# A fused S4D convolution and feed-forward kernel: the blocks of the convolution kernel dealt anew between two stretches of the program

## The chip, the cores and the metric

One core of a Trainium2 chip runs the program alone. The figure is device time in microseconds (us) of one execution, taken as the median of the executions timed; lower is better. Inside the core five engines work side by side, each through its own list of instructions in order: TensorE (PE in the profile) multiplies matrices, VectorE (DVE) and ScalarE (ACT) work element by element, GpSimd (POOL) here mostly issues transfers, and SyncE (SP) issues transfers only.

## The reference

The reference normalises an input `x` of 2048 positions by 576 channels, convolves every channel along the positions with a kernel of its own, adds a gated result to `x`, normalises again and runs a two-layer network with ReLU, 576 to 4608 to 576, all in float32:

```python
P = jnp.exp((A * dt[:, None])[:, :, None] * pos[None, None, :])
K = 2.0 * jnp.einsum("dn,dnl->dl", C, P).real       # 576 x 2048, from 128 modes a channel
...
y = jnp.fft.irfft(Uf * Kf[None, :, :], L2)[:, :, :L]
...
x = x + ga * (y + h * D_skip)
h = layernorm(x) * (1 + cb) + sb
x = x + gb * (jnp.maximum(h @ w1, 0) @ w2)
```

The six modulation vectors (`sa`, `ca`, `ga`, `sb`, `cb`, `gb`) come from one small matrix product.

## The kernel before

The 2048 positions are cut into four blocks of 512. Block `b` goes through the convolution (`conv(b)`, which works on spectra and takes in the earlier blocks' spectra), a normalisation and the feed-forward network, and its result is stored (`finish(b)`). The convolution kernel `K` is cut into the same four blocks of 512 positions; `conv(s)` needs `K`'s block `s` and its spectra of earlier blocks.

**Making a block of K.** The channels stand in 12 groups of 48, `h` = 0 to 11; groups 0 to 5 give half 0 of a block, groups 6 to 11 give half 1. For a group there are two factors: `W2` (128 modes by 48 channels by 32 x 2 values) and `W1` (128 modes by 48 by 16 x 2). Block 0 of K is the product of `W1` as first made (`W0` in `rest`) with `W2`. Another block needs `W0` turned by a complex factor: by `Z[:, 0]` for one block further, by `Z[:, 1]` for two blocks further. One such turn is `rot`: four VectorE instructions, on the lines 481, 483, 485 and 487. So block 1 is one turn from block 0, block 2 is another one turn from block 0, and block 3 is one turn from block 1 or from block 2.

**A visit.** Block 0 of K is made in the opening part, `first`, which also stores `W1`, `W2` and the powers `Z` of each group in DRAM. Blocks 1 to 3 are made later by `KGen.rest`, which is called twice. For each group it loads `W0`, `Z` and `W2` again (2400 KB), makes the turns that its plan asks for, lays them side by side in a tile `W1r`, and runs 96 small matrix products per group (line 515, tile `kps`) with `W2` as the stationary operand and all the turned `W1` as the moving one, 16 columns for each block of K. Two evictions on ScalarE (line 525, tile `ker`) follow, one per half of the 96. Here this is called a visit of a group. After six visits the rows of one half of the blocks in the plan are stored (`kd`).

**Where it runs.** The feed-forward network (`ffn`) of all four blocks is one loop of 144 steps `g`, 36 per block. A step has two halves: `first(g)`, 14 matrix products into `hps` (line 1326), and `second(g)`, 14 into the five accumulators `acc` (line 1352). Between them ScalarE takes the ReLU (`hh`, line 1331) and VectorE the low part (`hl`, line 1332), and the second half needs both. The weights `r` are loaded in each step; in the 36 steps of block 0 VectorE also splits them into a high and a low part (lines 1296, 1307, 1308) and SP writes the low parts to DRAM (`L1d`, `L2d`), from where the later blocks load them.

The other work is handed out between the halves. `step(g)` is called four times per step of the loop and draws from one Python generator per block: `block0` runs the first call of `rest` and then `conv(1)`, `block1` runs `finish(0)`, the second call of `rest` and `conv(2)`, `block2` runs `finish(1)` and `conv(3)`. A generator yields a weight for each piece of VectorE work (about its time in us), `None` for a piece of TensorE work (a quarter of a visit, one spectrum, one tile of the inverse), and -1 to end the hand-out of that call. Three limits apply: what has been handed out stays below `rate(block)` times the number of calls so far, with a `None` counted at 0.35 in block 0 and 0.7 in the others; the VectorE weight of four calls in a row stays below `room`; and no call gives more than 2.7 or two `None`. What is left at the end of a block is handed out at once. The scheduler below may still move an instruction a little within its engine's list.

**The plan before.** The first call of `rest`, in block 0's stretch of the loop, makes blocks 1, 2 and 3 of K for groups 0 to 5 (three turns, 48 columns) and block 1 for groups 6 to 11 (one turn, 16 columns), the two kinds in turn: 24 turns in 12 visits. The second call, in block 1's stretch, makes blocks 2 and 3 for groups 6 to 11: 12 turns in 6 visits. Lines below are those of the profile.

Of the kernel before, what the change touches and what calls it, by code (L numbers as in the profile page):

```python
# [10 lines left out]
F32 = mybir.dt.float32  # L11
# [7 lines left out]
P = 128  # L19
# [8 lines left out]
H = 48  # L28
# [21 lines left out]
class KGen:  # L50
# [403 lines left out]
    def rest(self, psum, plan):  # L454

        nc, k = self.nc, self.k
        v = nc.vector.tensor_tensor
        hs = list(plan)
        with ExitStack() as ctx:
            pt = k.pool(ctx, f"kr{len(hs)}", side="right")  # L460
            d = Kept(k.tc, nc.gpsimd).dma_start
# [39 lines left out]

            ke = {}

            def products(h, W1, W2):
                blocks = plan[h]
                na = 16 * len(blocks)
                if h % 6 == 0:
                    ke[h // 6] = pt.tile([P, na, 72], F32, tag=f"ke{na}", bufs=1, name=f"ker_{h}")
                for half in range(2):
                    ps = psum.tile([P, 6, na], F32, tag="cps", bufs=1, name="kps")  # L510
                    for q in range(6):
                        for dd in range(4):
                            ch = dd * 12 + 6 * half + q
                            for r in range(2):
                                nc.tensor.matmul(  # L515
                                    ps[32 * dd : 32 * dd + 32, q, :],
                                    W2[:, r, ch],
                                    W1[:, r, ch],
                                    start=(r == 0),
                                    stop=(r == 1),  # L520
                                )
# [14 lines left out]

            nxt = [load0(hs[0])]
            W2 = load2(hs[0])
            nxt.append(load0(hs[1]))
            for _ in range(1 if len(hs) == NH else 7):  # L540
                yield -1
            prev = iter(())
            for i, h in enumerate(hs):
                W0, Z = nxt.pop(0)
                if i + 2 < len(hs):
                    nxt.append(load0(hs[i + 2]))
                na = 16 * len(plan[h])
# [4 lines left out]
                if i + 1 < len(hs):  # L552
                    W2 = load2(hs[i + 1])
            yield from prev
# [11 lines left out]
class Body:  # L566
# [195 lines left out]
    def main(self, ctx, kg, hooks):  # L762
# [496 lines left out]
    def ffn(self, gens):  # L1259
# [102 lines left out]
        def step(g):  # L1362
# [110 lines left out]
    def rate(self, b):  # L1473
        return (2.15, 1.8, 1.4, 0.5)[b]

# [81 lines left out]
```

## Time and profile before

| what | value |
|---|---|
| median of 3 executions | 1338.84 us (1337.22 to 1343.99) |
| the profiled execution | 1346.28 us, of which its span 1344.5 us |
| mean granted TensorE clock in it | 0.934 |
| busy: PE, DVE, ACT, POOL | 1218.3, 895.8, 494.6, 162.5 us |
| moved by DMA | 345.85 MB, mean 257 GB/s |

The profiled execution's own time is 7.4 us over the median. The first eviction of the accumulators of a block (line 1436) marks the end of its stretch of the loop: it starts at 560.75 us for block 0, at 846.91 us for block 1 and at 1104.87 us for block 2. The loop's first ReLU is at 232.99 us. An engine's busy time is that in which it has an instruction running; a matrix product that waits between two others shows as idle time of PE, and the clock that PE was granted stands beside it.

### The profile page before, as it was taken

How to read it: one execution, taken by the hardware profiler on the slowest of the kernel's cores; microseconds unless marked ns; L12 is line 12 of the kernel's file. 1: busy time of each engine (PE TensorE's matmuls, PEld its weight loads, DVE VectorE, ACT ScalarE, POOL GpSimd, SP SyncE). 2: the span in 40 equal slices, each digit the busy share in tenths (PEclk: the TensorE clock that was granted, in tenths of full speed). 3: DMA queues.
4: the chain of work that ended last, by engine and by line, in shares of the span. 5: the costliest groups of instructions: out<-in, count | busy, mean ns of one | idle time of the engine just before them, and what ended most of it. 6: DMA issues, size and time to landing. Idle time of an engine off the chain costs nothing.

```text
span 1344.5 us, 26011 instructions
## 1 busy us (share of the span) xinstructions
PE 1218.3 (91%) x10720; PEld 963.8 (72%) x10720; DVE 895.8 (67%) x1324; ACT 494.6 (37%) x863; POOL 162.5 (12%) x260
## 2 busy tenths in 40 slices
PE   4565686889989998999999999999999999999997
PEld 3344564667768676777777887887888888888885
DVE  5999978997995999768658995467996221111112
ACT  5688523222223422622234225433323352323331
POOL 0656501001100100011001000100000000000000
PEclk9556767999999998999999999999999999999998
DMA  8567972987878877698889995867996667666661
GB/s 269 218 231 291 307 272 80 346 298 273 320 279 288 297 247 290 206 400 322 281 276 339 346 357 160 275 219 271 349 392 189 176 178 230 193 197 199 199 177 53
DMA packets 122379, 345.85 MB, mean 257 GB/s; under 512 B 23916, under 2 KB 24212, under 8 KB 111508
## 3 DMA queue, kind: packets, MB, share of 16 engines
q1 hardware_dynamic: 105364, 226.96, 50.9%
q0 software_dynamic: 16384, 115.85, 23.0%
q8 instruction: 84, 1.38, 0.4%
q10 hardware_dynamic: 512, 1.38, 0.3%
q14 instruction: 35, 0.29, 0.1%
HBM read 262.73 MB, written 81.40 MB: 256 GB/s over the span
## 4 chain that ended last, share of the span: by engine, by line
PE 72%; DVE 14%; DMA 7%; issue 4%; ACT 2%; POOL 1%; ACTq 0%; POOLq 0%; DVEq 0%; SPq 0%
PE acc L1352 29%; PE hps L1326 28%; DMA r<-in_w_dram 4%; PE ps_f L846 4%; PE kps L71 2%; PE ph L71 2%; PE kps L515 2%; PE ps_i L1053 2%; DVE W1r L483 2%; DVE T L481 2%; DMA L2d<-w 1%; DVE W1r L487 1%; DVE W1r L485 1%; DVE T L62 1%; DVE w L1296 1%
## 5 line engine op out<-in xcount | busy, mean ns | idle before, releaser
L1326 PE MATMUL hps<-xh,w 128*128 128x512 f32 x1152 | 393.6, 402 | 1.9 <-issue 1.1
L1352 PE MATMUL acc<-w,hh 128*128 128x512 f32 x1152 | 370.6, 403 | 12.9 <-ACT hh L1331 12.9
L1332 DVE SCALAR_TENSOR_TENSOR hl<-hps,hh 128x512 fp32r<-128x512 f32 x144 | 99.1, 688 | 310.1 <-ACT hh L1331 309.3
L1352 PEld LDWEIGHTS acc<-w,hh 128*128 128x128 f32 x1152 | 216.3, 189 | 60.7 <-ACT hh L1331 14.5
L1326 PEld LDWEIGHTS hps<-xh,w 128*128 128x128 f32 x1152 | 218.5, 190 | 50.2 <-issue 1.6
L1326 PE MATMUL hps<-xl,w 128*128 128x512 f32 x576 | 229.7, 400 | 0.1
L1352 PE MATMUL acc<-w,hl 128*128 128x512 f32 x576 | 223.0, 399 | 0.9 <-DVE hl L1332 0.9
L1331 ACT ACTIVATE hh<-hps 128x512 fp32r<-128x512 f32 x144 | 85.8, 596 | 289.7 <-PE hps L1326 289.4
L1301 ACT ACTIVATE w<-r 128x576 fp32r<-128x576 f32 x141 | 96.7, 686 | 231.0 <-PE acc L1352 219.5
L1291 ACT ACTIVATE w<-r 128x640 fp32r<-128x640 f32 x140 | 102.7, 733 | 92.8 <-DMA r<-in_w_dram 92.8
L1326 PEld LDWEIGHTS hps<-xl,w 128*128 128x128 f32 x576 | 109.3, 190 | 23.9 <-DVE xl L47 0.6
L1352 PEld LDWEIGHTS acc<-w,hl 128*128 128x128 f32 x576 | 107.9, 189 | 24.7 <-DVE hl L1332 2.1
L1326 PE MATMUL hps<-xs,w 128*128 128x512 f32 x288 | 98.6, 413 | 0.0
L71 PE MATMUL kps<-W,W 128*32 128x16 f32 x2304 | 39.9, 211 | 45.3 <-POOL W L68 28.1
L1032 DVE TENSOR_TENSOR Y<-Y,T 128x1152 f32<-128x1152 f32 x60 | 79.4, 1351 | 0.0
L71 PEld LDWEIGHTS kps<-W,W 128*32 128x32 f32 x2304 | 35.1, 144 | 59.0 <-POOL W L68 30.8
L847 ACT ACTIVATE Z<-ps_f 128x288 f32<-128x288 f32 x120 | 48.8, 408 | 70.2 <-PE ps_f L846 68.8
L515 PEld LDWEIGHTS kps<-W1r,W2r 128*32 128x32 f32 x3456 | 44.7, 113 | 37.7 <-issue 19.0
L515 PE MATMUL kps<-W1r,W2r 128*32 128x48 f32 (+2 forms) x3456 | 52.1, 201 | 14.6 <-ACT ker L525 9.3
L1471 POOL DMA_DIRECT2D out_dram<-x x16 | 8.7, 544 | 468.6 <-DVE x L1463 466.3
L1326 PEld LDWEIGHTS hps<-xs,w 128*128 128x128 f32 x288 | 54.0, 191 | 11.3
L1352 PE MATMUL acc<-hl,w 128*128 128x512 f32 x144 | 56.7, 394 | 0.0
(235 smaller groups left out, 1586.6 us busy)
## 6 DMA issues: line engine op xcount, KB each, us to landing
r<-in_w_dram SPq DMA_DIRECT2D x144, 320.0 KB, 7.3
r<-in_w_dram SPq DMA_DIRECT2D x144, 288.0 KB, 5.1
w<-L1d SPq DMA_DIRECT2D x108, 320.0 KB, 3.2
w<-L2d SPq DMA_DIRECT2D x108, 288.0 KB, 2.8
W2r<-W2d POOLq DMA_DIRECT2D x18, 1536.0 KB, 9.2
W2d<-W SPq DMA_DIRECT2D x12, 1536.0 KB, 8.6
Ua<-Ud POOLq DMA_DIRECT2D x15, 1152.0 KB, 9.6
W<-W1d POOLq DMA_DIRECT2D x18, 768.0 KB, 10.6
```

Of the source, the lines that this page charges most:

```text
L71: self.tc.keep_in_program_order(self.nc.tensor.matmul(*args, **kw))
L481: v(T, X, zi, op=ALU.mult)
L515: nc.tensor.matmul(ps[32 * dd : 32 * dd + 32, q, :], W2[:, r, ch], W1[:, r, ch], start=(r == 0), stop=(r == 1),)
L846: nc.tensor.matmul(o, fc[:, n2, c, :], src(n2), start=True, stop=True)
L847: ev = nc.scalar.activation(Z[:, n2, c], ps[:, :PC], AF.Copy)
L1032: v(y, y, T, op=op or ALU.add)
L1291: copy(g - 1)(w1[g][:, 0], r1[g], AF.Copy)
L1301: copy(g)(w[:, 0:D], r2[g], AF.Copy)
L1326: nc.tensor.matmul(ps, a, x, start=(i == 0), stop=(i == 13))
L1331: nc.scalar.activation(hh, ps, AF.Relu)
L1332: nc.vector.scalar_tensor_tensor(hl, ps, 0.0, hh, op0=ALU.max, op1=ALU.subtract)
L1352: nc.tensor.matmul(acc[i], a, x, start=(f == 0 and seen[i] == 1), stop=(f == NF - 1 and seen[i] == (3 if i < 4 else 2)),)
```

## The change

Which blocks of K are made in which stretch is dealt anew. Groups 0 to 5 now have blocks 1 and 3 made in block 0's stretch and block 2 in block 1's. Groups 6 to 11 keep block 1 in block 0's stretch and blocks 2 and 3 in block 1's. The groups are taken in their order, 0 to 11, in both calls. There are thus 18 turns in 12 visits in the first call, and 18 turns in 12 visits in the second: six turns move from block 0's stretch to block 1's, and the second call gets six visits more. The tiles are made alike for all visits: `W1r` has 32 columns and two buffers, of which 16 or 32 are used, and `ke` holds 32 columns, with two buffers in the first call and one in the second. The limits of the hand-out change too: `room` from 7.5 to 7.0 in block 0 and from 7.0 to 7.6 in block 1, `rate` from 2.15 to 1.8 and from 1.8 to 2.2.

```diff
         nc, k = self.nc, self.k
         v = nc.vector.tensor_tensor
-        hs = list(plan)
+        early = plan[0][0] == 1
...
-            def rots(h, W1, W0, Z):
-                blocks = plan[h]
-                a = [W1[:, :, :, 16 * i : 16 * i + 16] for i in range(len(blocks))]
-                if blocks[0] == 1:
-                    yield from rot(a[0], W0, Z, 0)
-                    if len(blocks) > 1:
-                        yield from rot(a[1], W0, Z, 1)
-                        yield from rot(a[2], a[0], Z, 1)
-                else:
-                    yield from rot(a[0], W0, Z, 1)
-                    yield from rot(a[1], a[0], Z, 0)
+            def rots(W1, W0, Z, n):
+                a = [W1[:, :, :, 16 * i : 16 * i + 16] for i in range(n)]
+                yield from rot(a[0], W0, Z, 0 if early else 1)
+                if n > 1:
+                    yield from rot(a[1], a[0], Z, 1 if early else 0)
...
-                    ke[h // 6] = pt.tile([P, na, 72], F32, tag=f"ke{na}", bufs=1, name=f"ker_{h}")
+                    t = pt.tile([P, 32, 72], F32, tag="ke", bufs=1 + early, name=f"ker_{h}")
+                    ke[h // 6] = t[:, :na]
...
-                                    W1[:, r, ch],
+                                    W1[:, r, ch, :na],
...
-            for i, h in enumerate(hs):
+            for h in range(NH):
...
-                bufs = 1 if len(plan[h]) != len(plan[hs[i - 1]]) else 2
-                W1 = pt.tile([P, 2, H, na], F32, tag=f"W1{na}", bufs=bufs, name=f"W1r_{h}")
-                yield from spread(rots(h, W1, W0, Z), prev, len(plan[h]))
+                W1 = pt.tile([P, 2, H, 32], F32, tag="W1", bufs=2, name=f"W1r_{h}")
+                n = len(plan[h // 6])
+                yield from spread(rots(W1, W0, Z, n), prev, n)
...
-            yield from kg.rest(
-                self.cps, {h: (1, 2, 3) if h < 6 else (1,) for h in (0, 6, 1, 7, 2, 8, 3, 9, 4, 10, 5, 11)}
-            )
+            yield from kg.rest(self.cps, ((1, 3), (1,)))
...
-            yield from kg.rest(self.cps, {h: (2, 3) for h in range(6, NH)})
+            yield from kg.rest(self.cps, ((2,), (2, 3)))
...
-            room = (7.5, 7.0, 7.0, 7.0)[g // NF] - sum(recent[-3:])
+            room = (7.0, 7.6, 7.0, 7.0)[g // NF] - sum(recent[-3:])
...
-        return (2.15, 1.8, 1.4, 0.5)[b]
+        return (1.8, 2.2, 1.4, 0.5)[b]
```

Three places show how the lists of instructions move. The lines of the changed program are 5 lower in the matrix products of a visit and their eviction (510, 520), and 8 lower from there on. `W1r` is the turned factor, `T` a scratch tile, `W_4` and `Zr` a loaded group, `w` and `r` feed-forward weights.

The first place is VectorE in block 0's stretch, from one `hl` to the next, while the groups are visited. Before, with a group of three turns:

```order
L1332 SCALAR_TENSOR_TENSOR hl<-hps,hh 128x512
L485 TENSOR_TENSOR W1r_4328<-W1r_4328,T 128x48x16
L487 TENSOR_TENSOR W1r_4328<-W1r_4328,T 128x48x16
L1307 TENSOR_TENSOR w_4400<-r_4081,w_4400 128x64
L481 TENSOR_TENSOR T<-W_4_3959,Zr_3960 128x1536
L1308 TENSOR_TENSOR w_4400<-r_4081,w_4400 128x512
L1296 TENSOR_TENSOR w_4295<-r_4213,w_4295 128x640
L483 TENSOR_TENSOR W1r_4328<-W_4_3959,Zr_3960 128x96x16
L483 TENSOR_TENSOR W1r_4328<-W1r_4328,Zr_3960 128x96x16
L485 TENSOR_TENSOR W1r_4328<-W1r_4328,T 128x48x16
L487 TENSOR_TENSOR W1r_4328<-W1r_4328,T 128x48x16
L1332 SCALAR_TENSOR_TENSOR hl<-hps,hh 128x512
```

Now, with a group of one turn:

```order
L1324 SCALAR_TENSOR_TENSOR hl<-hps,hh 128x512
L481 TENSOR_TENSOR T<-W_9_4205,Zr_4206 128x1536
L1300 TENSOR_TENSOR w_4522<-r_4143,w_4522 128x512
L1288 TENSOR_TENSOR w_4370<-r_4305,w_4370 128x640
L483 TENSOR_TENSOR W1r_4508<-W_9_4205,Zr_4206 128x96x16
L1299 TENSOR_TENSOR w_4701<-r_4307,w_4701 128x64
L485 TENSOR_TENSOR W1r_4508<-W1r_4508,T 128x48x16
L487 TENSOR_TENSOR W1r_4508<-W1r_4508,T 128x48x16
L1324 SCALAR_TENSOR_TENSOR hl<-hps,hh 128x512
```

Where seven instructions of turns stood between two `hl`, there are four. Over the stretch the turns are spread over the steps 0 to 15 where they took 0 to 17.

The second place is POOL's list at the start of block 1's stretch, behind the store of block 0's output, where the second call of `rest` loads its groups. Before, the loads begin with group 6 and end after six groups, 18 loads (the names of the DRAM tensors tell the group: `W2d_71` is group 6):

```order
L1471 DMA out_dram<-x_0_281 128x576 x4
L47 DMA W_6_6534<-W1d_83 128x1536
L47 DMA Zr_6535<-Zd_95 128x192
L47 DMA W2r_6538<-W2d_71 128x3072
L47 DMA W_7_6540<-W1d_84 128x1536
```

Now they begin with group 0 and go on to group 11, 36 loads, before `conv(2)`'s first:

```order
L1463 DMA out_dram<-x_0_281 128x576 x4
L47 DMA W_0_6502<-W1d_77 128x1536
L47 DMA Zr_6503<-Zd_89 128x192
L47 DMA W2r_6506<-W2d_65 128x3072
L47 DMA W_1_6508<-W1d_78 128x1536
```

The third place is ScalarE in block 1's stretch, where the visits pass from group 5 to group 6 and the tile of `ker`, which has one buffer here, is taken anew (`ker_6624`, then `ker_7532`). Now:

```order
L520 ACTIVATE ker_6624<-kps 128x16x6
L1323 ACTIVATE hh<-hps 128x512
L1283 ACTIVATE w_7439<-r_7410 128x640
L520 ACTIVATE ker_6624<-kps 128x16x6
L1293 ACTIVATE w_7570<-r_7230 128x576
L1323 ACTIVATE hh<-hps 128x512
L1283 ACTIVATE w_7574<-r_7520 128x640
L520 ACTIVATE ker_7532<-kps 128x32x6
L1293 ACTIVATE w_7703<-r_7412 128x576
```

The eviction into `ker_7532` has to wait until SP's two stores of `ker_6624` have landed. In the stretch before there is one `ker` tile only, and no such wait.

More of the change, by code (lines that the diff above doesn't have):

```diff
@@ L457, in rest @@
         v = nc.vector.tensor_tensor
-        hs = list(plan)
+        early = plan[0][0] == 1
         with ExitStack() as ctx:
-            pt = k.pool(ctx, f"kr{len(hs)}", side="right")
+            pt = k.pool(ctx, f"kr{early}", side="right")
             d = Kept(k.tc, nc.gpsimd).dma_start
@@ L535, in products @@
                         )
[L537 to L540, printed above, removed]
+            nxt = [load0(0)]
+            W2 = load2(0)
+            nxt.append(load0(1))
+            for _ in range(1 if early else 7):
                 yield -1
             prev = iter(())
-            for i, h in enumerate(hs):
+            for h in range(NH):
                 W0, Z = nxt.pop(0)
-                if i + 2 < len(hs):
-                    nxt.append(load0(hs[i + 2]))
-                na = 16 * len(plan[h])
-                bufs = 1 if len(plan[h]) != len(plan[hs[i - 1]]) else 2
-                W1 = pt.tile([P, 2, H, na], F32, tag=f"W1{na}", bufs=bufs, name=f"W1r_{h}")
-                yield from spread(rots(h, W1, W0, Z), prev, len(plan[h]))
+                if h + 2 < NH:
+                    nxt.append(load0(h + 2))
+                W1 = pt.tile([P, 2, H, 32], F32, tag="W1", bufs=2, name=f"W1r_{h}")
+                n = len(plan[h // 6])
+                yield from spread(rots(W1, W0, Z, n), prev, n)
                 prev = products(h, W1, W2)
-                if i + 1 < len(hs):
-                    W2 = load2(hs[i + 1])
+                if h + 1 < NH:
+                    W2 = load2(h + 1)
             yield from prev
```

2 lines of the change are left out of this document (1 added, 1 removed).

## The prediction

> **What bounds the kernel now.** I read the page's slices first, then a table of stretches, then the chain of waits.
>
> ```profile
> PE   4565686889989998999999999999999999999997
> DVE  5999978997995999768658995467996221111112
> PEclk9556767999999998999999999999999999999998
> ```
>
> From the middle on PE is full at full clock. The gaps lie before, in slices 8 to 17, and there DVE stands at 9 almost throughout. The table of stretches puts sizes on it; I cut it at the first ReLU (232), where the visits end (410, 670) and at the ends of the blocks' stretches (561, 847, 1105):
>
> ```profile
> core 0: us, PE busy (x) PEld busy (x) DVE busy (x) ACT busy (x) POOL busy (x), PEclk, DMA share, GB/s
> 232.00:410.00 178.00, 157.74 (x2610) 121.35 (x2610) 159.83 (x169) 42.82 (x79) 18.50 (x35) 0.94 0.80 290
> 410.00:561.00 151.00, 145.57 (x790) 112.45 (x789) 127.77 (x217) 55.30 (x108) 9.29 (x15) 0.98 0.80 283
> 561.00:600.00 39.00, 39.00 (x272) 31.92 (x272) 27.20 (x32) 16.42 (x28) 7.49 (x14) 1.00 0.88 333
> 600.00:670.00 70.00, 66.09 (x1267) 50.86 (x1266) 55.92 (x64) 18.95 (x39) 6.46 (x11) 1.00 0.86 309
> 670.00:847.00 177.00, 177.00 (x772) 141.30 (x771) 127.01 (x172) 68.09 (x125) 10.88 (x18) 1.00 0.83 291
> 847.00:1105.00 258.00, 258.00 (x1134) 209.32 (x1133) 165.26 (x231) 95.36 (x173) 12.35 (x22) 1.00 0.76 259
> ```
>
> Block 0's stretch takes 329 us, block 1's 286, block 2's 258, for the same 36 steps. In block 0's, PE idles 20.3 + 5.4 = 25.7 us, and its clock is granted at 0.94 and 0.98, which costs 157.74 x 0.06 + 145.57 x 0.02 = 12 us more. So 38 us of 329 are lost, and 291 are work at full clock. Block 1's stretch idles 3.9 us, block 2's not at all: PE bounds both. The chain of waits names what stands ahead of PE in block 0's visits, and shows the full pace of a half step in the last stretch:
>
> ```profile
> 375.30 0.74 DVE w L1296
> 376.04 1.67 DVE T L481
> 377.71 3.34 DVE W1r L483 x2
> 381.04 0.87 DVE W1r L485
> 381.91 0.87 DVE W1r L487
> ...
> 1302.01 3.17 PE acc L1352 x14
> 1305.18 3.17 PE hps L1326 x14
> ```
>
> The chain runs along DVE without a gap through turns and weight splits; `hl` waits behind them in DVE's list and holds PE's second half. A half step needs 3.17 us, a step 6.35.
>
> **The change, part by part.** *Six turns leave block 0's stretch.* Their price, from the groups by line over 232 to 562 us:
>
> ```profile
> L481 DVE TENSOR_TENSOR T<-W,Zr 128x1536 f32<-128x1536 f32 x18 | 31.5, 1748 | 0.0
> L483 DVE TENSOR_TENSOR W1r<-W,Zr 128x1536 f32<-128x1536 f32 x18 | 31.3, 1750 | 9.6 <-PE kps L515 9.6
> L487 DVE TENSOR_TENSOR W1r<-W1r,T 128x768 f32<-128x768 f32 x24 | 22.8, 948 | 0.0
> L485 DVE TENSOR_TENSOR W1r<-W1r,T 128x768 f32<-128x768 f32 x24 | 22.7, 947 | 0.0
> ```
>
> A turn is 1.75 + 1.75 + 0.95 + 0.95 = 5.4 us, six are 32.4 us of DVE. DVE's work in the stretch falls from 159.83 + 127.77 = 287.6 to 255.2 us. PE's 291 us do not fall, since the 12 visits stay: 16, 32 or 48 columns cost about the same.
>
> ```profile
> L515 PE MATMUL kps<-W1r,W2r 128*32 128x48 f32 x1152 | 18.4, 215 | 2.6 <-issue 2.4 <-DVE W1r L487 0.3
> L515 PE MATMUL kps<-W1r,W2r 128*32 128x16 f32 x1152 | 17.1, 189 | 8.1 <-ACT ker L525 5.3 <-issue 2.7
> L515 PE MATMUL kps<-W1r,W2r 128*32 128x32 f32 x1152 | 16.5, 200 | 3.9 <-ACT ker L525 3.9
> ```
>
> (These are six visits each, 48 and 16 columns in block 0's stretch, 32 in block 1's.) So the stretch can fall to 291 us at best, and the question is what of the 38 us stays. DVE would be busy 255 of some 307 us, 83%. The stretch 410 to 561 has DVE at 85% and loses 5.4 + 145.57 x 0.02 = 8.3 us of 151, 5.5%; 561 to 670 has it at 76% and loses 3.9 of 109, 3.6%. I take 5.5% of 291, 16 us, since 83% is nearer the first row. The stretch becomes 307: a gain of 22 us. Bounds: a loss of 30 us (the visits keep half of theirs because DVE's work comes in lumps of one turn) gives 8 us, a loss of 4 (block 1's) gives 34.
>
> The Trainium skill, TensorE: Matmul & The Clock Gate (Part 1: The HAM clock gate), says that PE's clock halves after an idle window of about 3.4 us and that a few us of work bring it back. The granted 0.94 and 0.98 beside the idle time agree in kind. By that rule the clock's 12 us are gone once no gap is longer than that; with only the 5.4 us of idle time of 410 to 561 left, the sum would come to 3 - 11 = -8 us.
>
> *Block 1's stretch gets six turns and six visits.* The turns, 32.4 us, raise DVE there from 27.20 + 55.92 + 127.01 = 210 to 242.5 us of about 310, 78%: still below PE, so they cost nothing by themselves, and at most what 85% cost above, 5.5% of 286 or 16 us, less the 3.9 already there: 12. The visits are different: nothing on PE is idle to hide them. A visit comes in four chunks, seen in the chain of waits:
>
> ```profile
> 610.87 0.65 PE kps L515 x44
> 611.52 1.80 PE acc L1352 x7
> 617.39 1.59 PE acc L1352 x7
> 618.98 1.10 PE kps L515 x77
> ```
>
> A chunk takes 0.65, and the seven products next to it 1.80 in place of 1.59: 0.86 for one, 3.4 a visit; a double one, with the same 0.21, is 1.31, 2.6 a visit. The stretch as a whole agrees. Block 2's 258 us hold 72 half steps, 228.5, and so 29.5 for `conv` and `finish`. Block 1's hold 73 (`first(36)` came after the cut) or 231.7, 29.5 and about 1.3 of block 0's late transposes; 286 less these leaves 23.5 for six visits, 3.9 with the idle time and 3.3 without. I take the whole, 24 us, because the waits for the eviction come with each visit. Bounds: 6 x 2.6 = 16 below, 24 + 12 = 36 above.
>
> *The new wait.* ScalarE's first eviction into the second `ker` tile waits for two stores. The transfers of this text, with the medians from issue to landing:
>
> ```profile
> r<-in_w_dram SPq DMA_DIRECT2D x144, 320.0 KB, 7.3
> r<-in_w_dram SPq DMA_DIRECT2D x144, 288.0 KB, 5.1
> w<-L1d SPq DMA_DIRECT2D x108, 320.0 KB, 3.2
> w<-L2d SPq DMA_DIRECT2D x108, 288.0 KB, 2.8
> W2r<-W2d POOLq DMA_DIRECT2D x18, 1536.0 KB, 9.2
> W<-W1d POOLq DMA_DIRECT2D x18, 768.0 KB, 10.6
> ...
> kd<-ker SPq DMA_DIRECT2D x12, 288.0 KB, 5.9
> ...
> Zr<-Zd POOLq DMA_DIRECT2D x18, 96.0 KB, 9.7
> ```
>
> A store lands 5.9 us after its issue. Between the two evictions PE has about a step of work, over 6.35 us. Behind the waiting eviction stand the copy of the next `w` and the next `hh`, for which PE would wait. I take 1 us, bounds 0 and 7 once.
>
> *Pace and tiles.* The tiles add no instruction. The order of the changed program ends `conv(1)` and `conv(2)` inside their stretches, so nothing is left to be drained behind the last step: 0. If 10 us of DVE work were left, PE would stand still that long.
>
> **The sum.** 0 - 22 + 24 + 1 = +3 us. Against the profiled execution, 1346.3 us (span 1344.5), it is 1349; that execution lies 7.4 over the median, and I carry the difference to the median: 1338.8 + 3 = **1342 us**. Blocks 2 and 3 and the opening part stay as they are.
>
> **The rivals.** *Faster: PE takes over block 0's stretch almost whole.* For it speaks that the chain there is DVE's, and that block 1 lost only 3.6% with DVE at 76%. With 4 us lost the gain is 34; with the visits at the double chunks' price block 1 pays 16, the new wait 1: -17, **1322 us**. Against it: even at 410 to 561, without visits, PE idled 5.4 us.
>
> *Slower: the transfers become the bound while groups are visited.* A visit loads 1536 + 768 + 96 = 2400 KB, 2.46 MB; a step moves 320 + 288 + 320 + 288 = 1216 KB, 1.25 MB. Now six visits of one turn fall into about five steps, at the end of block 0's visits and at the start of block 1's: 14.8 + 6.2 = 21 MB. PE needs 5 x 6.35 + 6 x 3.3 = 51.5 us for that. The rows above give 290 GB/s at a share of 0.80 and 309 at 0.86, so 362 and 359 when full: 58 us each time, 6.5 us short, 13 for both. A late `Zr` or `W2r` then stops DVE or PE at the head of its list. That gives 1342 + 13 = **1355 us**. It decides once the transfers stay below 21 / 51.5 = 408 GB/s. Against it:
>
> ```profile
> 572.00:582.00 10.00, 10.00 (x46) 8.29 (x45) 0.69 (x1) 3.48 (x6) 4.40 (x9) 1.00 1.02 402
> 592.00:602.00 10.00, 9.56 (x133) 7.45 (x131) 9.93 (x10) 1.91 (x3) 0.54 (x1) 1.00 1.02 402
> ```
>
> With `W`, `W2r` and weights together 402 GB/s were moved, nearly enough, and two groups are loaded ahead. The Trainium skill, DMA: Bandwidth & Descriptors (Where 436 GB/s comes from), puts the limit of one core's HBM at about 358 GB/s, by which this rival would hold; the 402 above is over it, so the rule does not bind here for 10 us at a time, and no row here shows it for 50.
>
> *The pace fails.* If turns are held back so long that `conv(2)`, which also feeds block 2's first step, ends late, PE stands still at 847: with 10 us left, 1342 + 10 = **1352 us**. The order speaks against it.
>
> **How the numbers follow.** Forecast (gain and price within 6.7 us of each other) 0.42, faster rival 0.28, transfers 0.25, pace 0.05. 0.5% of the median is 6.7 us, about what a measurement of this kernel can tell from no change. So faster 0.28, same 0.42, slower 0.30. The range runs from 1325 (near the faster rival; with both bounds at their best, -34 + 16, it would be 1321) to 1358 (the transfers' 1355 with a few us of the eviction's wait); the forecast's own range is 1334 to 1349.
>
> **What would show it.** Right: block 0's stretch at 300 to 312 us between its cuts, with DVE at 80 to 85% and a clock of 0.98 or more; block 1's at 306 to 318 with 12 visits of 3.3 to 4 us; blocks 2 and 3 as before. The faster rival shows as PE idle under 6 us in block 0's stretch. The transfers show as a DMA share of 1.0 over 40 us with DVE waiting for `Zr` or PE for `W2r`. A pause of ScalarE over 3 us before the seventh visit's first eviction in block 1 would price the new wait. I am wrong in kind if block 0's stretch stays above 320 us with DVE no longer full, or if block 1's grows by less than 14 us.

## The result, and the profile after

The changed kernel takes 1371.57 us (median of 4, 1370.42 to 1380.76) against 1338.18 us (1337.22 to 1343.99) before: a ratio of 1.0255, with a 95% interval of 1.0202 to 1.0309. It is slower by 33 us, where 1342 and no change were forecast, and it lies above the range. The profiled execution took 1380.76 us, its span 1378.7 us: 9 over the median, as that of before was 7 over its own.

The stretches end now, by the same marks as before (the first ReLU and the first eviction of the accumulators), at 234.8, 562.5, 877.6 and 1140.6 us. The table of stretches, before and after, one row each for block 0, 1 and 2. Before:

```profile
core 0: us, PE busy (x) PEld busy (x) DVE busy (x) ACT busy (x) POOL busy (x), PEclk, DMA share, GB/s
233.00:560.80 327.80, 302.19 (x3395) 233.18 (x3393) 287.20 (x385) 97.91 (x186) 27.48 (x50) 0.96 0.80 288
560.80:846.90 286.10, 282.19 (x2309) 224.07 (x2308) 210.13 (x267) 103.56 (x192) 24.83 (x43) 1.00 0.84 301
846.90:1104.90 258.00, 258.00 (x1134) 209.32 (x1133) 165.26 (x231) 95.36 (x173) 12.35 (x22) 1.00 0.76 259
```

After:

```profile
234.80:562.50 327.70, 305.17 (x3418) 237.11 (x3417) 260.56 (x365) 102.08 (x194) 27.52 (x50) 0.96 0.81 289
562.50:877.60 315.10, 299.74 (x3412) 232.15 (x3411) 235.81 (x282) 96.76 (x187) 34.40 (x61) 0.98 0.87 317
877.60:1140.60 263.00, 263.00 (x1160) 212.57 (x1159) 168.44 (x236) 100.79 (x182) 12.37 (x22) 1.00 0.75 257
```

VectorE's busy time in block 0's stretch fell by 26.6 us, to 80%, as meant, and the stretch is as long as before: 327.7 us. Block 1's is 29 us longer, block 2's 5.

Each stretch can be split into three parts: PE idle (length less busy), the clock (busy time times what is missing of the granted clock, summed over windows of 4 us, since a whole row rounds too much), and the rest, which is PE's work at full clock. This split is used for every run below; idle and clock together are called lost time.

| us | block 0: lost, work | block 1: lost, work | block 2: lost, work | sum of lost | sum of work |
|---|---|---|---|---|---|
| before | 35.3, 292.5 | 3.9, 282.2 | 0, 258.0 | 39.2 | 832.7 |
| after | 32.5, 295.2 | 20.3, 294.8 | 0, 263.0 | 52.8 | 853.0 |

Work grew by 20.3 us, 3.4 for each of the six added visits. (The marks shift some other work between the stretches: PE's counts in the rows grow by 23, 1103 and 26, together the 1152 of six visits. So block 2's 5 us belong to it: `conv(2)` ends later, and more of its transposes stand behind the mark.) Lost time grew by 13.6. Together that is 33.9 of the span's 34.2 us. So there are two questions: why block 0's lost time did not fall, and where block 1's 16 us come from.

The chain of waits through block 0's visits was VectorE's for the most part before. Now it is PE's own for the most part, with pauses under the name "issue", in which PE waits for nothing that the profile shows:

```profile
364.81 1.03 PE kps L510 x75
365.85 0.89 PE acc L1344 x3
366.74 0.89 PE kps L510 x61
367.63 3.32 issue
371.50 5.53 PE hps L1318 x14
...
408.13 3.17 PE hps L1318 x14
```

After a pause of 3.32 us the next half step takes 5.53 us where 3.17 is its pace, with the granted clock at 0.50 from 369.2 to 376.0 us: such a pause costs its length and a slow half step behind it. The groups of the page show the same word for the visits' products (last column: idle time of the engine before them, and what ended it). Before:

```profile
L515 PEld LDWEIGHTS kps<-W1r,W2r 128*32 128x32 f32 x3456 | 44.7, 113 | 37.7 <-issue 19.0
L515 PE MATMUL kps<-W1r,W2r 128*32 128x48 f32 (+2 forms) x3456 | 52.1, 201 | 14.6 <-ACT ker L525 9.3
```

After:

```profile
q8 instruction: 93, 1.52, 0.4%
...
L510 PEld LDWEIGHTS kps<-W1r,W2r 128*32 128x32 f32 x4608 | 58.5, 114 | 65.9 <-issue 46.5
L510 PE MATMUL kps<-W1r,W2r 128*32 128x32 f32 (+1 forms) x4608 | 68.7, 196 | 33.3 <-issue 21.5
...
r<-in_w_dram SPq DMA_DIRECT2D x144, 320.0 KB, 14.6
```

The queue "instruction" named here, q8, carries PE's own instructions. Before it had 84 packets; nine more came with 1152 more products (a visit's 96 show as 192 in the profile) and as many weight loads, 2304 instructions. A packet is 16 KB, so an instruction is 64 bytes and a packet holds 256, or 128 products with their weights; by that the 21440 products and weight loads of the page before fill 84 packets, as they do. A pause is counted here from one product's start to the next one's. The five pauses inside visits of block 0's stretch begin at 320.8, 336.1, 354.6, 367.4 and 390.6 us, and such packets at 320.9, 336.4, 355.6, 368.6 and 391.2, five of the eleven that begin between 320 and 395 us. Pauses over 0.9 us inside visits grew from 5.3 to 22.0 us over both stretches; PE's other waits fell in block 0's from 22.4 to 9.0. The last row is a second difference: a load of feed-forward weights lands 14.6 us after its issue where it took 7.3.

From this came the first theories. **A**: PE runs out of instructions in visits that stand close. **B**: the transfers are full while groups are visited, and loads come late. **C**: the new pace does the harm. Later **D** was added, the prediction's own: VectorE sets block 0's stretch.

### The profile page after: what moved, and what is told of

The parts are those of the page before. It is cut to its first block, busy times and chain, and to the rows that moved or that the text cites. A ratio compares the mean times of both kernels' runs of the same rounds, so it can differ in the third digit from the quotient of the medians.

```text
span 1378.7 us, 28379 instructions
## 1 busy us (share of the span) xinstructions
PE 1243.5 (90%) x11872; PEld 979.0 (71%) x11872; DVE 901.8 (65%) x1324; ACT 497.4 (36%) x875; POOL 172.4 (13%) x278
## 4 chain that ended last, share of the span: by engine, by line
PE 65%; DVE 10%; DMA 8%; issue 5%; ACT 1%; POOL 1%; POOLq 0%; SPq 0%; DVEq 0%; ACTq 0%
PE hps L1318 27%; PE acc L1344 26%; PE ps_f L838 4%; PE kps L510 3%; DMA Ua<-Ud 3%; DMA r<-in_w_dram 2%; DMA W2r<-W2d 1%; DVE T L1022 1%; PE ps_i L1045 1%; DVE Y L1024 1%; DMA x<-in_x_dram 1%; DMA kd<-ker 1%; DVE hl L1324 1%; PE ps_t L1140 1%; DVE T L481 1%
## 5 line engine op out<-in xcount | busy, mean ns | idle before, releaser
L1344 PE MATMUL acc<-w,hh 128*128 128x512 f32 x1152 | 376.9, 403 | 0.0
L1344 PE MATMUL acc<-w,hl 128*128 128x512 f32 x576 | 231.8, 403 | 2.4 <-DVE hl L1324 1.5
L1283 ACT ACTIVATE w<-r 128x640 fp32r<-128x640 f32 x140 | 102.5, 732 | 40.3 <-DMA r<-in_w_dram 38.7
L510 PEld LDWEIGHTS kps<-W1r,W2r 128*32 128x32 f32 x4608 | 58.5, 114 | 65.9 <-issue 46.5
L510 PE MATMUL kps<-W1r,W2r 128*32 128x32 f32 (+1 forms) x4608 | 68.7, 196 | 33.3 <-issue 21.5
L1344 PE MATMUL acc<-hh,w 128*128 128x512 f32 x144 | 57.4, 398 | 0.0
## 6 DMA issues: line engine op xcount, KB each, us to landing
r<-in_w_dram SPq DMA_DIRECT2D x144, 320.0 KB, 14.6
```

The costliest lines, as they stand in the source:

```text
L510: nc.tensor.matmul(ps[32 * dd : 32 * dd + 32, q, :], W2[:, r, ch], W1[:, r, ch, :na], start=(r == 0), stop=(r == 1),)
L1283: copy(g - 1)(w1[g][:, 0], r1[g], AF.Copy)
L1344: nc.tensor.matmul(acc[i], a, x, start=(f == 0 and seen[i] == 1), stop=(f == NF - 1 and seen[i] == (3 if i < 4 else 2)),)
```

## The experiments

All times are compared by their ratio to the runs of before on the same chip. Differences in us are differences of those ratios times 1338.8; the changed kernel stands at +34.1 on that scale. One profiled execution lies up to 9 us from its kernel's median, so of the splits only differences well over that, or those that times confirm, are used.

### Pace, transfers and products, one at a time

The old pace in the changed kernel:

```diff
-            room = (7.0, 7.6, 7.0, 7.0)[g // NF] - sum(recent[-3:])
+            room = (7.5, 7.0, 7.0, 7.0)[g // NF] - sum(recent[-3:])
...
-        return (1.8, 2.2, 1.4, 0.5)[b]
+        return (2.15, 1.8, 1.4, 0.5)[b]
```

> The changed plan with the old limits of the hand-out (room 7.5 and 7.0, rate 2.15 and 1.8); nothing is left out. Theory A (PE runs out of instructions inside a visit, because the visits stand close and its instruction blocks of 16 KB come too slowly): the old limits do not draw the visits apart in block 0's stretch, so the pauses inside visits stay at 15 us or more in sum (22 us in the changed kernel) and the time at 1355 to 1380. Theory B (transfers are full while groups are visited): about the same as A. Theory C (the new pace does the harm): back to 1340 to 1350 with pauses inside visits under 8 us.

Measured 1396.57 us, 1.0410 [1.0369, 1.0451]: 21 us slower than the changed kernel and outside what any of the three theories gave. Block 0's and 1's stretches are 326.3 and 299.1 us, but block 2's is 297.6, with 28.3 lost: `conv(2)` is not ended and is drained with PE waiting. C falls: the new pace is what this plan needs.

Half of the `W2` loads left out:

```diff
-                if h + 1 < NH:
+                if h + 1 < NH and h % 2:
                     W2 = load2(h + 1)
```

> The changed kernel with the factor W2 loaded for every second group only; the next group uses the tile that is there, so its rows of K are not the reference's. PE's instructions are the same; 6 loads of 1536 KB fewer in each of the two stretches, 9.4 MB of some 46. Theory A: the pauses inside visits stay above 12 us in sum and the time falls by less than 12 us, to 1360 to 1372. Theory B: the DMA share while groups are visited falls under 0.8, the pauses inside visits under 6 us, and the time by 20 us or more, to under 1352.

Measured 1358.06 us, 1.0128 [1.0092, 1.0164]: 17 us faster than the changed kernel, which lies between what A and B gave. The pauses inside visits stay at 20.3 us, the other waits over 0.9 us fall from 17.9 to 3.9, and lost time from 52.8 to 33.3. So late transfers have a price of their own.

Half of the products left out:

```diff
-                            for r in range(2):
+                            for r in range(1):
```

> The changed kernel with half of the products of each visit left out (the imaginary half of the sum), so that a visit is 48 products and 192 PE instructions in place of 384; the transfers are the same. K is not the reference's. The products themselves save 24 x 1.3 = 31 us of PE's work. Theory A: the pauses inside visits fall under 6 us in sum and the clock in the visits rises to 0.97 or more, so the time falls by 31 + 16 or more, to 1310 to 1328. Theory B: pauses in the visits of the same total, since the loads come no sooner; time 1335 to 1345.

Measured 1336.57 us, 0.9969 [0.9942, 0.9997]: 38 us faster. Work falls by 20.5 and 19.8 us for twelve half visits each, so a whole visit is 3.4 us of PE's work: the price again. Not one pause inside visits is left, but other waits over 0.9 us grow from 17.9 to 45.1. The waits of its block 0's visits say which (us in all, times, longest):

```profile
ACT w L1283 <- DMA r<-in_w_dram: 48.5, 13, 10.9
...
PE kps L510 <- ACT ker L520: 17.2, 4, 6.9
```

ScalarE stands 48.5 us at the copy of weights that have not landed; the eviction of the visit stands behind it in its list, and PE waits for the eviction. With less to do in a visit, PE reaches the transfers' limit: lost time is 56.0, no less than with all products.

The visits alone: twelve in a row with nothing else, and twelve more beside large loads, in a kernel that does nothing else of the task.

> No part of the reference is computed: 12 visits of 96 products back to back on PE with constant operands and four buffers for the result, first with no transfer running, then again while loads of 1536 KB and 320 KB run. Theory A: PE pauses about once per 256 instructions already without transfers, so a visit takes 4 to 6 us in place of the 2.6 of its products, and somewhat more under the loads. Theory B: 2.6 us a visit without transfers, with no pause over 0.5 us, and pauses of 2 to 3.5 us only under the loads.

The chain of waits of this kernel (start, length, what), first without loads, then with them:

```profile
53.28 1.75 issue
55.03 1.98 PE quiet L45 x125
57.01 1.47 issue
```

```profile
96.76 4.49 issue
101.25 1.99 PE loud L45 x122
103.24 4.21 issue
107.45 1.98 PE loud L45 x125
109.43 1.75 issue
```

PE runs one packet of instructions (some 125 of 128 products are recorded) and pauses, again and again: 3.45 us a packet, 62.7 us for twelve visits or 5.2 each; beside loads the pauses reach 5 us and a visit takes 7.3. (PE's granted clock was 0.50 here.) So A's mechanism exists: close products ask for instructions faster than these come, and loads slow that down. Whether it costs the changed kernel its time was still to be shown.

### Spreading the visits

At most one piece of PE's work (a quarter of a visit) per call of the hand-out, in the steps with visits:

```diff
-            while done[0] < target and v < min(room, 2.7) and pe < 2:
+            while done[0] < target and v < min(room, 2.7) and pe < (1 if g < 2 * NF and g % NF < 19 else 2):
```

> The changed kernel, but while groups are visited (the first 19 steps of blocks 0 and 1) a call of the hand-out gives at most one piece of TensorE work in place of two, so that the quarters of a visit stand further apart among the feed-forward products. Nothing is left out; bytes and products are the same. Theory A (instruction blocks come too slowly inside close visits): the pauses inside visits fall from 22 us to under 8, the granted clock there rises to 0.97 or more, and the time falls by 10 to 25 us, to 1347 to 1362. Theory B (transfers are full): as many bytes in about the same time, so the time stays within 6 us of the changed kernel's 1371.6.

> The kernel with the quarters of the visits apart, and W2 loaded for every second group only (the other group's rows of K are not the reference's). If pauses inside visits (A) and late loads (B) are two separate costs, both gains add: the half loads alone gave 13.5 us, so this is 10 to 16 us under the kernel with the quarters apart, and its PE idle time in the two stretches is under 12 us. If there is one cost only, it is within 5 us of that kernel.

> The changed kernel with the quarters of a visit apart and the groups of one and of two turns alternating (0, 6, 1, 7 and so on) in both stretches, with a tile of W1r and of ker for each kind, so that the new wait for a store of ker is gone too. Nothing is left out. Theory A and B both expect a gain over the kernel with the quarters apart, since neither visits nor loads bunch: 4 to 10 us; with pauses inside visits under 5 us it can reach 1340 to 1352. Faster than the kernel before, under 1332, only if block 0's stretch comes down to 305 us.

Measured: spread 1377.89 us, 1.0265 [1.0227, 1.0304], a miss; with half of `W2` 1371.04, 1.0221 [1.0184, 1.0257]; with the two kinds of groups in turn 1373.82, 1.0233 [1.0200, 1.0266]. In the spread kernel the pauses inside visits fell from 22.0 to 4.1 us and lost time in blocks 0 and 1 from 52.8 to 29, but block 2's stretch was 289.0 with 21.4 us lost: the spread had delayed `conv(2)`, which was then drained, as a row of its table of stretches shows behind the mark:

```profile
849.00:870.00 21.00, 10.65 (x22) 5.43 (x21) 15.15 (x37) 4.86 (x11) 0.00 (x0) 0.57 0.09 29
```

That left it open whether A's 24 us were gained and given back, or only pushed behind the mark. So the spread was done again with limits meant to end `conv(2)` in time: in block 0's stretch alone, in both, and in both with the kinds in turn.

```diff
-            room = (7.0, 7.6, 7.0, 7.0)[g // NF] - sum(recent[-3:])
+            room = (7.4, 7.6, 7.0, 7.0)[g // NF] - sum(recent[-3:])
...
-            while done[0] < target and v < min(room, 2.7) and pe < 2:
+            while done[0] < target and v < min(room, 2.7) and pe < (1 if g % NF < (19, 0, 0, 0)[g // NF] else 2):
...
-        return (1.8, 2.2, 1.4, 0.5)[b]
+        return (1.95, 2.2, 1.4, 0.5)[b]
```

This is the edit to the changed kernel for block 0 alone. For both stretches `room` is 8.4 and `rate` 2.6 in block 1, with 19 in the second place of the other tuple, and the seven calls that the second use of `rest` lets pass before its first visit are left out.

> The changed kernel with at most one piece of TensorE work per call of the hand-out in the first 19 steps of block 0's stretch only, and with rate 1.95, room 7.4 there, rate 2.2, room 7.6 in block 1, so that conv(1) and conv(2) end where they end in the changed kernel. In the spread kernel the stretches of blocks 0 and 1 became 11.6 and 11.7 us shorter and block 2's 26 us longer, since its last products of conv(2) stood behind the boundary with TensorE idle. Theory A (TensorE runs out of instructions in visits that stand close): block 0's stretch 312 to 318 us, block 1's 313 to 317, block 2's 262 to 266, so 1357 to 1364 us. If the spread only moves a loss from one stretch to the next: 1368 to 1375.

> The spread in both stretches (one TensorE piece per call in their first 19 steps), and conv(2) brought to its end earlier: the visits of block 1's stretch begin seven calls of the hand-out sooner, with rate 2.6 and room 8.4 there (block 0: 1.95 and 7.4). Theory A, with the drain of conv(2) as a cost of its own: block 0's stretch 312 to 318 us, block 1's 300 to 306, block 2's 262 to 275: 1343 to 1358 us. If the price of the six added visits is TensorE's work and not its missing instructions, block 1's stretch is 312 or more and the time stays at 1362 or more. If VectorE is then too full in block 1's stretch, block 2's stays at 280 or more.

> As the run before it in this list, and the groups of the two kinds taken in turn (0, 6, 1, 7, ...) in both stretches, with a tile of its own for each kind of W1r and of ker. The two spread runs before differed by 4.1 us in favour of the alternating order. Theory A: 3 to 8 us below the run with the spread in time, so 1338 to 1352 us. If the transfers of the groups of one turn were the cost that the alternating order takes away, the DMA share over 20 us stays below 1.0 in the visits and the difference is 8 to 14 us.

Measured 1372.93 us, 1.0225 [1.0170, 1.0280]; 1381.87, 1.0305 [1.0256, 1.0354]; 1375.54, 1.0250 [1.0206, 1.0294]. None is faster than the changed kernel by more than its interval. But only the first ends `conv(2)` in time: block 2's stretch is 263.1 us there, and 275.1 and 275.3 in the other two, which lose 9.9 and 10.1 of it. So the first is the clean test of A, for block 0's stretch: its pauses inside visits fell there from 14.7 to 6.1 us, the other waits rose from 9.0 to 20.8, and lost time is 35.8 where it was 32.5. With the spread in both, pauses inside visits are 13.4 us where they were 22.0, and the other waits 26.5 where they were 17.9: the sum is the same. In block 0's visits ScalarE again stands 38.6 us at weights that have not landed, and PE behind it (the waits of the kernel with the spread in both, without the alternating order):

```profile
ACT w L1283 <- DMA r<-in_w_dram: 38.6, 7, 8.2
...
PE kps L510 <- ACT ker L520: 14.2, 4, 5.9
```

So A as *the* cause falls for block 0's stretch: fewer pauses gave other waits, not time. For block 1's it stays open, since no run has the visits there spread and `conv(2)` in time. Two more tries were made on the kernel before. Its six visits in block 1's stretch were handed out in one piece each instead of in quarters, and its block 0's visits were spread:

```diff
-                        if q == 2:
+                        if q == 2 and len(hs) == NH:
                             yield None
...
-                    yield None
+                    if half or len(hs) == NH:
+                        yield None
```

(`len(hs) == NH` holds in the first use of `rest` only.)

> The kernel before, in which the six visits of block 1's stretch are handed out whole, each visit in one piece, where they came in four quarters. Nothing else changes: bytes, turns and products are the same. Theory A: PE now pauses inside these visits, 1.5 to 3.5 us in each of four to six, where it had no such pause; the time rises by 4 to 14 us. Theory B: no pause inside the visits and a change under 4 us, if anything faster, since fewer switches between the two kinds of products are paid (0.21 us each).

```diff
-            while done[0] < target and v < min(room, 2.7) and pe < 2:
+            while done[0] < target and v < min(room, 2.7) and pe < (1 if g < 19 else 2):
```

> The kernel before with one change: at most one piece of TensorE work per call of the hand-out in the first 19 steps. There TensorE had 5.3 us of pauses inside visits and 22.4 us of other waits in block 0's stretch, most of them for VectorE. Theory A: the 5.3 us go, with their clock 4 to 9 us, if VectorE leaves them free: 1330 to 1336. If VectorE alone sets that stretch: the pauses go and the waits for it grow by as much, 1336 to 1344, with block 0's stretch at 324 or more. If conv(1), which ends two steps later, is late at the boundary: over 1345.

Measured 1346.26 us, 1.0038 [1.0016, 1.0060], and 1348.62, 1.0033 [1.0005, 1.0062] (ten executions, one of which took 4085.55 us for a reason that is not known). Close visits cost 5 us, within A's range, but with one pause of 1.9 us where A had four to six. The spread lost 4 us: block 0's stretch is 10 us shorter in its profile and block 1's 14 longer, since `conv(1)` then came late, as the third case of the expectation had it.

### VectorE or transfers, in the kernel before

The change's relief of VectorE by itself: in the kernel before, the third turn is left out in five visits, and its pieces are still counted.

```diff
-                        yield from rot(a[2], a[0], Z, 1)
+                        if h == 0:
+                            yield from rot(a[2], a[0], Z, 1)
+                        else:
+                            yield from (1.75, 1.75, 0.95, 0.95)
...
-                W1 = pt.tile([P, 2, H, na], F32, tag=f"W1{na}", bufs=bufs, name=f"W1r_{h}")
+                if na < 48 or h == 0:
+                    W1 = pt.tile([P, 2, H, na], F32, tag=f"W1{na}", bufs=bufs, name=f"W1r_{h}")
+                    big = W1 if na == 48 else big if i else None
+                else:
+                    W1 = big
```

> The kernel before with the third turn left out in five of its six visits of three turns (the tile keeps the first one's; the pieces are still counted by the hand-out, so nothing else moves): 20 instructions, 27 us less on VectorE in block 0's stretch, the visits and the loads as they were. This is the change's relief of VectorE alone. Theory D (VectorE's full list sets that stretch, as the prediction had it): the stretch 10 to 25 us shorter, 1316 to 1331 us. Theory B (late transfers set it: ScalarE stands at the copy of weights that have not landed, and the eviction and the ReLU stand behind it): the waits for VectorE go and others come in their place, 1334 to 1343 us.

The transfers by themselves, with one `W2` for two visits:

```diff
-                if i + 1 < len(hs):
+                if i + 1 < len(hs) and i % 2:
                     W2 = load2(hs[i + 1])
```

> The kernel before with W2 loaded for every second visit only (a visit uses the tile of the visit before): 9.4 MB less in block 0's stretch, 4.7 in block 1's, VectorE's work and the visits as they were. Theory B: 8 to 18 us shorter, 1323 to 1333 us, and ScalarE's waits for the loaded weights, 58 us in block 0's visits, fall below 25. Theory D: VectorE is as full as before, 1336 to 1342 us.

Both:

> The two edits of the runs before it in this list together. If either VectorE or the transfers alone set the stretch, this is as fast as that one's run, within 4 us. If each stands behind the other: 20 to 30 us shorter than before, 1311 to 1321, more than both gains together.

And the changed kernel with half of the products and half of the `W2` loads:

> The changed kernel with half of each visit's products left out and W2 loaded for every second group only. The half products alone gave 1336.6 us, the half W2 alone 1358.1, against 1371.6. With the half products the pauses inside visits were gone and 45 us of other waits stood in the two stretches. If those are late transfers (theory B), 12 to 22 us less: 1315 to 1325. If they are not, 1332 to 1338. The lost time by theory A and B together falls below 15 us in each stretch.

| kernel | time, us | ratio | against its base |
|---|---|---|---|
| before, five turns fewer | 1334.94 | 0.9954 [0.9929, 0.9979] | -6 |
| before, half of `W2` | 1347.76 | 1.0058 [1.0037, 1.0080] | +8 |
| before, both | 1321.97 | 0.9856 [0.9819, 0.9892] | -19 |
| after, half of `W2` | 1358.06 | 1.0128 [1.0092, 1.0164] | -17 |
| after, half of the products | 1336.57 | 0.9969 [0.9942, 0.9997] | -38 |
| after, both | 1316.26 | 0.9826 [0.9782, 0.9869] | -57 |

Five turns less, 27 us by the times of their instructions and 23.4 of VectorE's busy time in the stretch, are worth 6 us (3 to 10), not the 10 to 25 of theory D. Half of `W2` is worth nothing there, and even costs 8 us, against theory B alone: ScalarE's waits for loaded weights fall in the visits from 58.3 to 37.2 us, not under 25, and why it costs is not settled (in its profile one load of weights lands 12.14 us after its issue, and PE stands 8 us behind it). Both together are worth 19, some 21 more than the two apart. With VectorE relieved, the same half of `W2` is worth 13 us in the kernel before, and 17 and 19 in the changed one; with half of `W2`, VectorE's relief is worth 27. The stretches of block 0, for the three kernels in the table's order:

```profile
227.50:543.30 315.80, 300.88 (x3398) 231.94 (x3398) 263.76 (x366) 98.42 (x187) 27.44 (x50) 0.98 0.84 300
```

```profile
230.60:560.00 329.40, 301.03 (x3395) 232.91 (x3393) 287.36 (x385) 98.65 (x186) 24.38 (x44) 0.96 0.74 258
```

```profile
228.20:536.90 308.70, 298.79 (x3398) 230.19 (x3398) 263.93 (x366) 98.26 (x188) 24.43 (x44) 0.99 0.79 276
```

(The executions shown lie 8, 4 and 3 us under their kernels' medians.) In the last one PE idles 9.9 us and the clock is 0.99. Relieving one limit alone gives little; only with both relieved does the stretch, at 308.7 us, come near to the 307 that the prediction had for VectorE's relief alone.

In the changed kernel without half of its products and of `W2`, lost time is 29.6 us; with the products and without half of `W2` it was 33.3, in one profile each. So the denser products cost their 3.4 us a visit and at most a few us of pauses beyond that, once the transfers have room.

## Why the prediction was wrong, point by point

**The -22 for block 0's stretch failed, and with it the sum.** The failed step is the reading of the 38 lost us as VectorE's. I saw VectorE at 90% and its chain of turns, and took a second stretch with VectorE at 85% as the measure of what would stay. (Of the ten slices that I named DVE stands at 9 in seven.) The seven us of the chain of waits that I showed are VectorE's without a gap, but they are a fragment. Over the visits, 233 to 410 us, 45% of that chain are turns and weight splits on VectorE, and 19% are transfers waited for, in three pieces (start, length, what):

```profile
235.81 10.36 DMA r<-in_w_dram
...
287.57 9.87 DMA r<-in_w_dram
...
386.97 13.54 DMA L2d<-w
```

So a second limit stood in the chain itself, the last piece right behind my fragment. It also stood in the waits of ScalarE in the visits of block 0's stretch in the kernel before, which I did not read:

```profile
ACT w L1291 <- DMA r<-in_w_dram: 58.3, 11, 11.2
```

Before the change, ScalarE already stood 58 us at weights not yet landed. By itself that sum proves no limit: with five turns fewer and all loads it is 30.2 us. That the two limits stand behind each other is shown by the times of the four kernels, of which VectorE's relief alone gives 6 us, half of `W2` alone none, and both 19. In the changed kernel the relief did take away what it was meant to, since PE's other waits fell in this stretch from 22.4 to 9.0 us; but pauses inside visits rose from 5.3 to 14.7, and the clock costs about 10 us as before. The term measures 6 us for five turns in the kernel before, and 3 (of lost time, in one profile each, less 2.7 of work) in the change. My lower bound of 8 was too high. The turns themselves were priced too high as well: six were to take 32.4 us off VectorE and took 26.6. The text's own test, "wrong in kind if block 0's stretch stays above 320 us with DVE no longer full", is what happened: 327.7 us at 80%.

**The +24 for block 1's stretch was right in its work and too small in its waits.** 3.4 us of PE's work a visit was one of the two prices, and the split (20.3 for six) and the half products (40.3 for twenty-four halves) both give it. I took 3.9 to cover the waits, some 3.6 us for the six. They came to 16.4 us more lost time in that stretch, in pauses inside visits (7.3 us), other waits and the clock behind both. That the stretch's 315 us lie inside the 306 to 318 that I gave is in part luck: the 5 us that the mark put into block 2's, which I had at zero, would have made it 320.

**The new wait (+1) was right.** The changed kernel's waits around the seventh visit (us in all, times, longest):

```profile
ACT ker L520 <- DMA kd<-ker: 3.3, 1, 3.3
```

ScalarE stands 3.3 us at the store, over the 3 that I named, and PE idles 0.88 us there.

**The pace (0) was right**, and the old pace costs 21 us more. That it was needed I had only from the order.

**The rivals.** The transfers were the nearest. I priced them at 13 us from 21 MB in 51.5 us; half of `W2` is worth 17 to 19 in the changed kernel. I put that price on top of a gain of 22 which the same transfers held down, so its 1355 was still 17 short. The first half of my sign of it, a DMA share of 1.0 over 40 us, came, at a rate just under the 408 GB/s that I had named as the point from which this rival decides. The rows show 40 us with visits in the changed kernel, in the kernel before, and in the first spread kernel with the two kinds of groups in turn (block 1's stretch begins at 562.5, 560.8 and 542.3 us):

```profile
578.00:618.00 40.00, 32.69 (x669) 25.32 (x668) 26.50 (x21) 7.95 (x16) 5.75 (x11) 0.92 1.03 406
578.00:618.00 40.00, 37.32 (x432) 29.79 (x431) 33.72 (x29) 10.89 (x20) 3.55 (x7) 1.00 0.98 381
578.00:618.00 40.00, 39.83 (x794) 30.15 (x795) 31.71 (x28) 11.03 (x22) 4.95 (x10) 1.00 1.02 400
```

The second half of the sign, DVE waiting for `Zr` or PE for `W2r`, hardly came: 6.4 and 0.4 us in the first row, where DVE waited 9.1 for `Zr` before. PE idles 7.3 us in the first row, 6.4 of them in pauses inside visits, and 0.2 in the last, where three and a half visits run in place of three beside transfers as full. So a full share alone does not stop PE; in the changed kernel it stands together with close visits.

The limit of about 358 GB/s for one core's HBM, which the prediction took from the Trainium skill, DMA: Bandwidth & Descriptors (Where 436 GB/s comes from), does not bind here. The 406 and 400 GB/s over 40 us are above it.

The faster rival needed PE to take over once VectorE had room, which the run with five turns fewer excludes.

**The clock.** I expected 0.98 or more in block 0's stretch and got 0.96. By the rule that the prediction cited (the Trainium skill, TensorE: Matmul & The Clock Gate, Part 1: The HAM clock gate), a clock that halves after about 3.4 us of idle time, the pauses should mostly not cost clock. The changed kernel's chain shows half pace behind a shorter one:

```profile
336.32 2.40 issue
339.36 2.00 PE acc L1344 x4
```

Shortly after 2.40 us of pause four products take 2.00 us, where 14 take 3.17, and the granted clock is 0.50 from 338.5 to 341.9 us. Here the measurement differs from the rule's window.

**What stays open**: how block 1's 16 us divide between missing instructions and late loads. With half of `W2` lost time there falls from 20.3 to 10.0 us (one profile each), with its pauses inside visits at 7.1 where they were 7.3. With the visits spread it falls to 6.3, and with the kinds in turn besides to 2.3, but then `conv(2)` is late and block 2's stretch loses 21 us, so how much of that is a gain and how much is only put off is not shown. The order of the groups by itself, without the spread, was not run, though the change altered it too.

## What to carry to other kernels

A stretch in which one engine is 90% busy can have a second limit at the same height; before pricing the relief of the first, read the chain of waits over the whole stretch and not a piece of it, and the waits of every engine that stands between (here ScalarE, standing at loads), and count on a small part of the relief only unless those are small. Lost time is worth splitting from work: six visits added to a stretch where PE is full cost at least their work, and any gain elsewhere has to be larger than that. A burst of small matrix products has two prices besides PE's time, the loads that it asks for and its own instructions.

## What had not been expected of the hardware

PE's instructions come in packets of 16 KB on a DMA queue, 256 instructions each (93 packets for 23744 products and weight loads in the changed kernel). In the kernel of visits alone, small products back to back use up a packet in 1.98 us at a granted clock of 0.50 and go on 3.45 us after its start, or up to 7 us beside large loads; the profile calls the wait "issue". Where products of 0.23 us stand between them, as in the kernel before in block 1's stretch, no such pause is seen. And behind pauses of 2.4 and 3.3 us in the changed kernel the granted clock was 0.50 for 3.4 and 6.8 us; the half step behind the longer one took 2.4 us more.
